# An earlier gather for the feed-forward's first group, another ring place for its first scratch, and alternating engines at each group's end

## The chip, the cores and the metric

One core of a Trainium2 chip runs the whole program in one launch. The metric is the device time of one execution in microseconds, the median of the runs shown; smaller is better. The core's engines are TensorE (PE in the profile, with PEld for its weight loads), VectorE (DVE), ScalarE (ACT), GpSimd (POOL) and the queue of SyncE (SP), which issues most of the transfers. TensorE's granted clock has two levels, 2.4 GHz (1.0 in the rows) and 1.2 GHz (0.5).

## The reference

Three stages follow each other:

```python
# 1. clustered attention: 2 batches, 8 heads, 768 positions, width 64
mask = q_assign[:, :, :, None] == k_assign[:, :, None, :]     # same nearest centroid
attn = softmax(where(mask, q @ k.T / 8, -1e9));  x = attn @ v  # -> 1536 tokens of 512
# 2. mixture of 8 experts, one per token
idx = argmax(xn @ en.T / tau);  gate = softmax(...)[idx]
out[idx == e] = gate * (relu(x[idx == e] @ w1[e]) @ w2[e])     # 512 -> 1024 -> 512
# 3. feed-forward with a rational function
h = x @ w_in;  P = a0 + a1*h + a2*h^2 + a3*h^3;  Q = 1 + |b0|*|h| + |b1|*h^2
y = (P / (Q + 1e-6)) @ w_out                                    # 512 -> 2048 -> 512
```

Tokens don't influence one another in stages 2 and 3, so their order there is free as long as each row ends at its place in the output.

## The kernel before

**Attention** fills the span up to about 300 us. It also writes every token's row and expert logits to the DRAM tensor `xd`, and `route` counts each token's rank within its expert.

**Experts.** Each expert e has 256 rows (`cap`); expert e's tokens are fetched by rank with indirect transfers (`load_x`, L842). The loop over `steps` runs eight experts in four steps (e, p) each: `expert_in` (L958), `expert_relu`, and `expert_out` of the step before (L981 to L983). After an expert's last `expert_out`, ACT scales its result into `ysb` (L987), POOL adds the token number (L71) and SP stores it to `ys_d` (L990), two stores per expert, 128 rows each. The last expert's steps are (7, 0) to (7, 3).

**Slots.** `positions` sorts the tokens by expert without gaps and computes for each of the 12 blocks of 128 sorted tokens which row of `ys_d` each token has (`slot_all`), which lanes must not be written (`never_all`), and which tokens are left over (`ovf_all`): those past rank 256 of their expert, and those among the first 512 whose expert is not covered by the first group's gather. If any is left over, a loop at the end (L1206 on) computes it again in a general way; its count is read once (`left`, L1164).

**Feed-forward.** Three groups of four blocks (512 tokens), each in 16 steps (g, f). `gather` (L996) fetches a block's rows from `ys_d` by an indirect transfer of POOL's queue; a transfer waits for the stores to the rows that its slice of `ys_d` holds. The first group's four gathers are issued after step (7, 0); `transpose_y` (L1010, copies L1012 and L1013) of its blocks stands in steps (7, 2) and (7, 3), between `expert_in` and `expert_out`. Step (0, 0) begins before the last `expert_out`. In each later step TensorE does `ff_in` (L1026, 12 matmuls) of that step and `ff_out` (L1150 to L1152, 12 matmuls) of three steps before. Between them the rational function goes around three engines: `poly_1` (ACT L1049 to L1051, DVE L1052 and L1054, POOL L1053), `poly_2` one step later (ACT L1125 and L1126, DVE L1127 to L1129), `poly_3` (ACT L1137, and L1138 on POOL in the first group, on DVE in the others). `ff_in`'s results have two PSUM places from step (0, 2) on, and L1054 is the last reader of one, so `ff_in` of step (0, f) waits for L1054 of step (0, f-2). The scratch tile `Bt` has one place: ACT's L1051 of a step waits for DVE's L1128 of the step before.

**The ring of weights.** Eight places (`ck0` to `ck7`) hold chunks of weights, split into two parts by ACT (L110) and DVE (L113). Chunk n lies in place n modulo 8. Place 4 held expert 7's first half of `w1` (chunk 28, last read in step (7, 1)) and takes the third chunk of `w_in` (chunk 36) in steps (0, 1) to (0, 3). Place 6 held expert 7's first half of `w2` (chunk 30, last read by `expert_out` of (7, 1)) and takes the fourth chunk of `w_in` (chunk 38) from step (0, 6) on. The parts of the feed-forward's chunks are made by `wide_part`, two in odd and one in even steps, after `poly_3` of the step before. Step (0, 0) runs while the experts' pools are still open, so its scratch (`spare`) is taken from the ring.

**Order.** The work is ordered by hand (`manual_schedule`); each engine runs its instructions in that order, so a waiting instruction holds all behind it on its engine.

Of the kernel before, what the change touches and what calls it, by code (L numbers as in the profile page):

```python
# [16 lines left out]
ALU = mybir.AluOpType  # L17
# [4 lines left out]
P = 128  # L22
# [6 lines left out]
def attention_moe_kernel(ctx: ExitStack, tc: tile.TileContext, kqT, vp, centroids,  # L29
                         emb, tau, w1, w2, w_in, w_out, pa, pb, out, cap=256, dbg=None):  # L30
# [7 lines left out]
    pe, act, dve, pool, sp = nc.tensor, nc.scalar, nc.vector, nc.gpsimd, nc.sync  # L38
# [4 lines left out]
    E, DM, F = w1.shape  # L43
# [10 lines left out]
    NEVER = 1 << 20  # L54
# [29 lines left out]
    oh_all = const.tile([P, NBT, E], F32, name="oh_all")  # L84
# [3 lines left out]
    slot_all = const.tile([P, NBT], I32, name="slot_all")  # L88
    never_all = const.tile([P, NBT], F32, name="never_all")
    ids = const.tile([P, E * 2], F32, name="ids")  # L90
    rank_all = stage.tile([P, NBT], F32, name="rank_all", bufs=1)
# [28 lines left out]
    def prep_f32(key, src, tag):  # L120

        raw = stage.tile([P, 4, 512], F32, name="wraw", tag="wraw")
        sp.dma_start(raw, src)
        yield
        ck = new_chunk(key, tag)
        for i in range(4):
            split_to(ck, i, raw[:, i], act, dve)
            yield
# [16 lines left out]
    RING = 8  # L145


    plan = []
# [3 lines left out]
    plan = [prep_f32(key, src, n % RING) for n, (key, src) in enumerate(plan)]  # L152
# [434 lines left out]
    n = len(units)  # L587
# [246 lines left out]
    GB = 4  # L834
# [42 lines left out]
    def positions():  # L877
        def big(name, n=E):
            return mo.tile([P, NBT, n], F32, name=name, bufs=1)

        def small(name, n=E):
            return mo.tile([P, n], F32, name=name, bufs=1)

        dve.tensor_copy(ids, row_tok)
        empty = small("pem", E * 2)
        dve.tensor_scalar(empty, ids, 0.0, float(NEVER), op0=ALU.is_equal, op1=ALU.mult)
        dve.scalar_tensor_tensor(ids, ids, -1.0, empty, op0=ALU.add, op1=ALU.add)
        pi = pX.tile([P, KC, P], F32, name="px2")[:, 0, 0:E]
        for e in range(E):
            pe.matmul(pi[:, e:E], onesb, cum[:, e:e + 1].to_broadcast([P, E - e]), start=(e == 0),  # L890
                      stop=(e == E - 1))
        inc = small("pin")
        dve.tensor_copy(inc, pi)
        yield
        more = small("pmo")
        dve.tensor_scalar(more, inc, -1.0, float(cap), op0=ALU.mult, op1=ALU.add)
        dve.tensor_tensor(more[:, 1:E], more[:, 1:E], inc[:, 0:E - 1], op=ALU.add)
        ge, gd, ex, sl = big("pge"), big("pgd"), big("pex", 1), big("psl", 1)
        dve.tensor_tensor(ge, tok.unsqueeze(2).to_broadcast([P, NBT, E]),
                          inc.unsqueeze(1).to_broadcast([P, NBT, E]), op=ALU.is_ge)  # L900
        dve.tensor_tensor(gd, ge, more.unsqueeze(1).to_broadcast([P, NBT, E]), op=ALU.mult)
        yield
        dve.tensor_reduce(ex, ge, axis=AX.X, op=ALU.add)
        dve.tensor_reduce(sl, gd, axis=AX.X, op=ALU.add)
        ex, sl = ex[:, :, 0], sl[:, :, 0]
        dve.tensor_tensor(sl, sl, tok, op=ALU.add)
        dve.tensor_scalar(slot_all[:, 0:GB], sl[:, 0:GB], float((E - 1) * cap - 1), None, op0=ALU.min)
        dve.tensor_scalar(slot_all[:, GB:], sl[:, GB:], float(ROWS - 1), None, op0=ALU.min)
        yield

        dve.scalar_tensor_tensor(sl, ex, -float(cap), sl, op0=ALU.mult, op1=ALU.add)
        dve.tensor_scalar(never_all, sl, float(cap), float(NEVER), op0=ALU.is_ge, op1=ALU.mult)
        dve.tensor_scalar(ex[:, 0:GB], ex[:, 0:GB], float(E - 1), float(NEVER), op0=ALU.is_ge, op1=ALU.mult)
        dve.tensor_tensor(never_all[:, 0:GB], never_all[:, 0:GB], ex[:, 0:GB], op=ALU.max)
        yield

        ovf_all = big("pov", 1)[:, :, 0]
        dve.tensor_scalar(ovf_all, rank_all, float(cap), None, op0=ALU.is_ge)
        dve.tensor_scalar(sl, rank_all, inc[:, E - 2:E - 1], float(GB * P), op0=ALU.add, op1=ALU.is_lt)
        dve.tensor_tensor(sl, sl, oh_all[:, :, E - 1], op=ALU.mult)  # L920
        dve.tensor_tensor(ovf_all, ovf_all, sl, op=ALU.max)
        yield
        ovb = mo.tile([P, NBT], BF16, name="povb", bufs=1)
        dve.tensor_copy(ovb, ovf_all)
        yield
        cnt = pX.tile([P, KC, P], F32, name="px2")[:, 0, 0:NBT]
        pe.matmul(cnt, onesb, ovb, start=True, stop=True)
        dve.tensor_copy(cnt_i[:, 0:NBT], cnt)
        tot = small("ptot", 1)
        dve.tensor_reduce(tot, cnt, axis=AX.X, op=ALU.add)  # L930
        dve.tensor_copy(cnt_i[:, NBT:], tot)

        dve.tensor_scalar(dst_left, ovf_all, -float(NEVER), float(NEVER), op0=ALU.mult, op1=ALU.add)
        dve.tensor_tensor(dst_left, dst_left, tok, op=ALU.add)
# [57 lines left out]
    def gather(gi, tb):  # L992
        k = gi * GB + tb
        y = rows.tile([P, W], F32, name="y", bufs=4)
        n = (E if gi else E - 1) * cap
        pool.indirect_dma_start(out=y, out_offset=None, in_=ys_d[0:n, :],  # L996
                                in_offset=bass.IndirectOffsetOnAxis(ap=slot_all[:, k:k + 1], axis=0),
                                bounds_check=n - 1, oob_is_err=False)
        x2["y", k] = y
# [31 lines left out]
    def cuts(gi, fb):  # L1031

        if (gi, fb) in ((0, 0), (NG - 1, F2B - 1)):
            return [slice(0, GT // 2), slice(GT // 2, GT)]
        return [slice(0, GT)]

    def poly_1(gi, fb):
        h = hs[gi, fb]
        if (gi, fb) == (0, 0):
            if fb == 0:  # L1040
                n = (len(plan) + 4) % RING
                hs["spare"] = pools[n].tile([P, 2, 4, 512], F32R, name="spare", tag=f"ck{n}")
            A, Bt, Ct = (hs["spare"][:, fb, k].bitcast(F32) for k in range(3))
        else:
            A = ro.tile([P, GT], F32, name="A")
            Bt = bt.tile([P, GT], F32, name="Bt", bufs=1)
            Ct = ro.tile([P, GT], F32, name="Ct", bufs=3)
        for c in cuts(gi, fb):
            act.activation(A[:, c], h[:, c], AF.Abs)  # L1049
            act.activation(Ct[:, c], h[:, c], AF.Identity, scale=ab[:, 3:4], bias=ab[:, 2:3])  # L1050
            act.activation(Bt[:, c], A[:, c], AF.Identity, scale=bb[:, 1:2], bias=bb[:, 0:1])  # L1051
            dve.tensor_tensor(Ct[:, c], Ct[:, c], h[:, c], op=ALU.mult)  # L1052
            (dve if (gi, fb) == (NG - 1, F2B - 1) else pool).tensor_tensor(Bt[:, c], Bt[:, c], A[:, c], op=ALU.mult)  # L1053
            dve.scalar_tensor_tensor(Ct[:, c], Ct[:, c], ab[:, 1:2], h[:, c], op0=ALU.add, op1=ALU.mult)  # L1054
        hs[gi, fb] = (A, Bt, Ct)

    with tc.manual_schedule():
# [6 lines left out]
        for i, (e, p) in enumerate(steps):  # L1064
# [24 lines left out]
            if e == E - 1:  # L1089
                if p == 0:  # L1090
# [4 lines left out]
                    for tb in range(GB):  # L1095
                        gather(0, tb)
        ff_in(0, 0)
        poly_1(0, 0)
        expert_out(*steps[-1])
        passed.add(("out", *steps[-1]))  # L1100
# [11 lines left out]
    gs, op = {}, {}  # L1112
# [4 lines left out]
    def scatter(y, dst, n):  # L1117
        pool.indirect_dma_start(out=outs[n][:, :], out_offset=bass.IndirectOffsetOnAxis(ap=dst, axis=0),  # L1118
                                in_=y, in_offset=None, bounds_check=NT - 1, oob_is_err=False)
# [21 lines left out]
    def ff_out(gi, fb):  # L1141
        ghi, glo = gs.pop((gi, fb))
        if fb == 0:
            op[gi] = [pR.tile([P, DM], F32, name=f"pr{tb}") for tb in range(GB)]
        w = chunks["wo", fb // 4]
        k = fb % 4
        for tb in range(GB):
            s_ = slice(tb * P, (tb + 1) * P)
            o = op[gi][tb]
            pe.matmul(o, ghi[:, s_], w[:, 0, k, :], start=(fb == 0), stop=False)  # L1150
            pe.matmul(o, ghi[:, s_], w[:, 1, k, :], start=False, stop=False)  # L1151
            pe.matmul(o, glo[:, s_], w[:, 0, k, :], start=False, stop=(fb == F2B - 1))  # L1152
            if fb == F2B - 1:
                b = gi * GB + tb
                if tb % 2 == 0:
                    op["o"] = yraw[0].tile([P, 2, DM], F32, name="yraw", bufs=3)
                y = op["o"][:, tb % 2]
                if tb >= 2:
                    dve.tensor_scalar(y, o, -1.0, None, op0=ALU.mult)
                else:  # L1160
                    act.activation(y, o, AF.Copy, scale=-1.0)
                scatter(y, dst_all[:, b:b + 1], b)
# [3 lines left out]
    with tc.manual_schedule():  # L1166
        dve.memset(qc, QC)
        steps = [(gi, fb) for gi in range(NG) for fb in range(F2B)]
        for i, (gi, fb) in enumerate(steps):
# [4 lines left out]
            if gi + 1 < NG and fb in (4, 6, 8, 10):  # L1174
                tb = (fb - 4) // 2
# [145 lines left out]
```

## Time and profile before

| | |
|---|---|
| median of 3 runs | 788.43 us (787.19 to 793.78) |
| the profiled execution | 789.97 us, span 788.2 us, mean granted clock 0.977 |
| PE busy | 740.8 us, 94% |
| PEld busy | 646.4 us, 82% |
| DVE busy | 595.9 us, 76% |
| ACT busy | 566.9 us, 72% |
| POOL busy | 351.9 us, 45% |

The shares are means over stages. The last 350 us belong to the experts' second half and the feed-forward; there PE is busy almost without a break, and what it waits for is what counts. A row of the timeline gives start, duration, engine, line, operation, output and inputs, and in brackets the engine's idle time before it and what ended that; a row with x8 is eight instructions of one kind in a stretch without others between them.

### The profile page before, as it was taken

The numbers are of one execution on the slowest core, as the hardware profiler recorded it, in microseconds if no ns is written. First come the engines' busy times: TensorE is split into PE (matmuls) and PEld (weight loads), VectorE is DVE, ScalarE is ACT, GpSimd is POOL, SyncE is SP. The second block draws the span as 40 slices with busy tenths as digits, with TensorE's granted clock in tenths as the row PEclk, the third lists the DMA queues.
The fourth block names the chain that finished last, engine by engine and source line by source line (L and its number), as shares of the span: only waits on it lengthen the run. The fifth ranks groups of instructions, "written<-read, shape, count | busy, mean of one in ns | idle before, by whom it ended". The sixth has DMA issues, their size and how long they took to land. (4 is left out here: it accounts for less than half of the span.)

```text
span 788.2 us, 12616 instructions
## 1 busy us (share of the span) xinstructions
PE 740.8 (94%) x4292; PEld 646.4 (82%) x4292; DVE 595.9 (76%) x1117; ACT 566.9 (72%) x1132; POOL 351.9 (45%) x448
## 2 busy tenths in 40 slices
PE   5999999999969976999999998989999999999995
PEld 4799999989869965889999997868888888888883
DVE  7788888889868984976765654488977878787874
ACT  3788888888868863776775554478887777777773
POOL 7497888778766522011111012156544431242211
PEclk9999999999999996999999999989999999999998
DMA  5566775877877342899655565222100200010001
GB/s 152 151 195 179 213 218 170 257 215 219 282 190 212 108 134 63 278 308 318 228 195 200 186 188 188 81 67 93 31 0 1 82 14 14 1 54 1 1 0 58
DMA packets 48313, 109.22 MB, mean 139 GB/s; under 512 B 6921, under 2 KB 10505, under 8 KB 48242
## 3 DMA queue, kind: packets, MB, share of 16 engines
q1 hardware_dynamic: 45042, 97.74, 39.8%
q0 software_dynamic: 3200, 10.60, 4.3%
q8 instruction: 36, 0.59, 0.3%
q14 instruction: 35, 0.29, 0.1%
HBM read 76.06 MB, written 18.99 MB: 121 GB/s over the span
## 5 line engine op out<-in xcount | busy, mean ns | idle before, releaser
L1053 POOL TENSOR_TENSOR Bt<-Bt,A 128x512 f32<-128x512 f32 x46 | 59.7, 1297 | 149.8 <-ACT Bt L1051 149.8
L446 DVE TENSOR_TENSOR plo<-pt,phi 128x384 fp32r<-128x384 f32 x160 | 88.0, 550 | 23.5 <-ACT phi L436 21.0
L436 ACT CAST phi<-pt 128x384 fp32r<-128x384 f32 x160 | 76.8, 483 | 35.7 <-PE pt L428 34.5
L428 PE MATMUL pt<-ident,pr 128*128 128x128 f32 x576 | 97.2, 278 | 2.6 <-DVE plo L446 2.3
L413 DVE TENSOR_REDUCE nm<-ps 128x1 f32<-128x768 f32 x96 | 91.3, 951 | 9.7 <-PE ps L411 9.2
L1026 PE MATMUL pg<-x2hi,ck 128*128 128x512 f32 x368 | 94.0, 398 | 3.2 <-DVE Ct L1054 3.2
L113 DVE TENSOR_TENSOR ck<-wraw,ck 128x512 fp32r<-128x512 f32 x128 | 82.9, 699 | 14.5 <-ACT ck L110 14.5
L419 ACT ACTIVATE pr<-ps,nm 128x768 f32<-128x768 f32 x96 | 87.5, 912 | 1.8 <-DVE nm L413 1.2
L1026 PEld LDWEIGHTS pg<-x2hi,ck 128*128 128x128 f32 x368 | 70.1, 191 | 19.3 <-DVE Ct L1054 3.6
L428 PEld LDWEIGHTS pt<-ident,pr 128*128 128x128 f32 x576 | 72.7, 142 | 14.8 <-DVE plo L446 6.7
L1150 PE MATMUL pr<-ck,ghi 128*128 128x512 f32 x192 | 76.2, 397 | 0.0
L1152 PE MATMUL pr<-ck,glo 128*128 128x512 f32 x192 | 75.4, 393 | 0.0
L110 ACT CAST ck<-wraw 128x512 fp32r<-128x512 f32 x128 | 71.2, 623 | 5.6 <-DMA wraw<-in_w_dram 5.5
L1151 PE MATMUL pr<-ck,ghi 128*128 128x512 f32 x192 | 75.1, 391 | 0.0
L410 PE MATMUL ps<-KA,QA 128*128 128x384 f32 x192 | 73.7, 384 | 1.0 <-ACT pr L419 0.6
L456 PE MATMUL po_acc<-phi,vhl 128*128 128x384 f32 x192 | 74.5, 388 | 0.0
L958 PE MATMUL ph<-xhi,ck 128*128 128x256 f32 x512 | 73.2, 286 | 0.7 <-ACT xhi L945 0.7
L958 PEld LDWEIGHTS ph<-xhi,ck 128*128 128x128 f32 x512 | 68.9, 194 | 3.7 <-ACT xhi L945 1.1
L411 PE MATMUL ps<-KB,QB 128*128 128x384 f32 x192 | 66.3, 345 | 5.0 <-DMA QB<-ot 3.4
L852 POOL TENSOR_TENSOR gss<-gss,half 128x2 f32<-128x2 f32 x8 | 5.8, 722 | 143.7 <-ACT px L851 143.7
L457 PE MATMUL po_acc<-plo,vhl 128*128 128x384 f32 x192 | 65.6, 342 | 0.0
L1127 DVE SCALAR_TENSOR_TENSOR Bt<-Bt,A 128x512 f32<-128x512 f32 (+1 forms) x48 | 32.7, 682 | 39.8 <-ACT A L1126 39.7
(252 smaller groups left out, 1848.7 us busy)
## 6 DMA issues: line engine op xcount, KB each, us to landing
wraw<-in_w_dram SPq DMA_DIRECT2D x32, 1024.0 KB, 6.2
words<-in_w_in_dram SPq DMA_DIRECT2D x16, 512.0 KB, 6.0
wf_d<-wz SPq DMA_DIRECT2D x32, 256.0 KB, 3.5
words<-in_w_out_dram SPq DMA_DIRECT2D x16, 512.0 KB, 5.0
yraw<-wf_d SPq DMA_DIRECT2D x16, 512.0 KB, 4.0
kq<-in_kqT_dram SPq DMA_DIRECT2D x16, 384.0 KB, 5.3
ys_d<-ysb SPq DMA_DIRECT2D x16, 260.0 KB, 4.7
v<-in_vp_dram SPq DMA_DIRECT2D x16, 192.0 KB, 5.3
```

The source lines that it names most:

```text
L113: el.tensor_tensor(ck[:, 1, i], src, ck[:, 0, i].bitcast(F32), op=ALU.subtract)
L413: dve.tensor_reduce(nm, ps[:, :, :HS], axis=AX.XY, op=ALU.max, negate=True)
L419: act.activation(pr.rearrange("p (a s) -> p a s", a=2), ps[:, :, :HS], AF.Exp, bias=nm[:, 0:1], accum_out=st["sum", u][:, qb:qb + 1])
L428: pe.transpose(t[:, j, :], st["P", u][j][:, kb * P:(kb + 1) * P], ident)
L436: act.copy(phi, tv)
L446: dve.tensor_tensor(plo, tv, phi.bitcast(F32), op=ALU.subtract)
L456: pe.matmul(o, w, phi, start=(kb == 1), stop=False)
L958: pe.matmul(ph[:, f2, :], w[:, wx, k, c0:c0 + P], x[:, k, :], start=(i == 0), stop=(i == len(ops) - 1))
L1026: pe.matmul(ph, w[:, wx, k, c0:c0 + P], x[:, k, :], start=(i == 0), stop=(i == len(ops) - 1))
L1150: pe.matmul(o, ghi[:, s_], w[:, 0, k, :], start=(fb == 0), stop=False)
L1151: pe.matmul(o, ghi[:, s_], w[:, 1, k, :], start=False, stop=False)
L1152: pe.matmul(o, glo[:, s_], w[:, 0, k, :], start=False, stop=(fb == F2B - 1))
```

## The change

The first group is gathered from the rows of the first six experts instead of the first seven; the clamp of its slots, its lanes that must not be written and the left-over tokens follow (a token of the first 512 whose expert is 6 or 7 is now left over; three small DVE instructions more). The scratch of step (0, 0) lies in ring place 6 instead of 4. At the end of each group the four blocks of output are negated by ACT, DVE, ACT, DVE instead of ACT, ACT, DVE, DVE.

```diff
-        dve.tensor_scalar(slot_all[:, 0:GB], sl[:, 0:GB], float((E - 1) * cap - 1), None, op0=ALU.min)
+        dve.tensor_scalar(slot_all[:, 0:GB], sl[:, 0:GB], float((E - 2) * cap - 1), None, op0=ALU.min)
...
-        dve.tensor_scalar(ex[:, 0:GB], ex[:, 0:GB], float(E - 1), float(NEVER), op0=ALU.is_ge, op1=ALU.mult)
+        dve.tensor_scalar(ex[:, 0:GB], ex[:, 0:GB], float(E - 2), float(NEVER), op0=ALU.is_ge, op1=ALU.mult)
...
-        dve.tensor_scalar(sl, rank_all, inc[:, E - 2:E - 1], float(GB * P), op0=ALU.add, op1=ALU.is_lt)
-        dve.tensor_tensor(sl, sl, oh_all[:, :, E - 1], op=ALU.mult)
-        dve.tensor_tensor(ovf_all, ovf_all, sl, op=ALU.max)
+        for e in (E - 2, E - 1):
+            dve.tensor_scalar(sl, rank_all, inc[:, e - 1:e], float(GB * P), op0=ALU.add, op1=ALU.is_lt)
+            dve.tensor_tensor(sl, sl, oh_all[:, :, e], op=ALU.mult)
+            dve.tensor_tensor(ovf_all, ovf_all, sl, op=ALU.max)
...
-        n = (E if gi else E - 1) * cap
+        n = (E if gi else E - 2) * cap
...
-                n = (len(plan) + 4) % RING
+                n = (len(plan) + 6) % RING
...
-                if tb >= 2:
+                if tb % 2:
                     dve.tensor_scalar(y, o, -1.0, None, op0=ALU.mult)
                 else:
                     act.activation(y, o, AF.Copy, scale=-1.0)
```

## Rows read from the trace of the kernel before

**Rows 1.** Waits of TensorE, 440 us to the end: us in total, times, longest.

```profile
PE pg L1026 <- DVE Ct L1054: 3.2, 1, 3.2
PE px L1010 <- DMA y<-ys_d,slot_all: 2.5, 1, 2.5
```

**Rows 2.** Timeline of TensorE, steps (7, 2) and (7, 3) of the experts.

```profile
483.38 1.10 PE L958 MATMUL ph<-xhi,ck 128*128 128x256 f32 x8
...
488.94 1.97 PE L1010 MATMUL px<-ident,y 128*128 128x128 f32 x8 [2.54 <-DMA y<-ys_d,slot_all]
...
494.24 1.10 PE L958 MATMUL ph<-xhi,ck 128*128 128x256 f32 x8
...
500.76 2.02 PE L1026 MATMUL px<-x2hi,ck 128*128 128x512 f32 x8
```

**Rows 3.** Stretches: us, busy PE, PEld, DVE, ACT, POOL, granted clock, DMA, GB/s.

```profile
489.00:492.00 3.00, 3.00 (x12) 2.71 (x13) 1.20 (x3) 1.64 (x4) 0.00 (x0) 0.50 0.44 143
...
520.00:526.00 6.00, 5.29 (x13) 4.13 (x13) 4.92 (x8) 5.15 (x9) 3.74 (x4) 0.50 0.00 0
...
349.00:356.00 7.00, 5.79 (x38) 4.98 (x38) 6.87 (x18) 5.46 (x11) 0.00 (x0) 1.00 0.68 215
```

**Rows 4.** Timeline of TensorE: `ff_in` of (0, 4), (0, 5) and (0, 10).

```profile
520.71 3.78 PE L1026 MATMUL pg<-x2hi,ck 128*128 128x512 f32 x8 [3.21 <-DVE Ct L1054]
...
529.00 2.02 PE L1026 MATMUL pg<-x2hi,ck 128*128 128x512 f32 x8
...
557.25 2.02 PE L1026 MATMUL pg<-x2hi,ck 128*128 128x512 f32 x8
```

**Rows 5.** Timeline of POOL: the first gather.

```profile
483.67 1.13 POOL L996 DMA_INDIRECT y<-ys_d,slot_all  x1 [9.03 <-DMA yraw<-wf_d]
```

**Rows 6.** Timeline of SP's queue: the stores of experts 5 and 6.

```profile
455.48 0.81 SPq L990 DMA_DIRECT2D ys_d<-ysb  x2
...
478.02 1.02 SPq L990 DMA_DIRECT2D ys_d<-ysb  x2
```

**Rows 7.** The page's DMA issues: count, KB each, median us from issue to landing.

```profile
ys_d<-ysb SPq DMA_DIRECT2D x16, 260.0 KB, 4.7
```

**Rows 8.** The gathered tile: ns min/median/max, first and last start; then us to landing.

```profile
L996 POOL DMA_INDIRECT y<-ys_d,slot_all x12: 998/1319/1348, 483.7 to 648.7; - x12
...
DMA to landing us min/median/max: 3.7/3.9/5.2
```

**Rows 9.** Timeline of DVE and of TensorE around the left-over count.

```profile
338.79 0.19 DVE L920 TENSOR_TENSOR psl<-psl,oh_all 128x12 f32<-128x12 f32 x1
...
346.84 1.89 DVE L113 TENSOR_TENSOR ck<-wraw,ck 128x512 fp32r<-128x512 f32 x3 [3.09 <-ACT ck L110]
...
351.35 0.66 PE L943 MATMUL px<-ident,xr 128*128 128x128 f32 x4 [1.22 <-DVE ptot L930]
```

**Rows 10.** Timeline of ACT: the first casts into place 4.

```profile
514.61 1.14 ACT L110 CAST ck<-yraw 128x512 fp32r<-128x512 f32 x2 [2.20 <-POOL glo L1138]
```

**Rows 11.** Timeline of POOL: `poly_3` of (0, 0).

```profile
513.15 1.43 POOL L1138 TENSOR_TENSOR glo<-spare,ghi 128x256 fp32r<-128x256 f32 x2
```

**Rows 12.** Timeline of DVE, steps (0, 1) to (0, 3), and L1054 of (0, 8).

```profile
515.26 1.29 DVE L113 TENSOR_TENSOR ck<-yraw,ck 128x512 fp32r<-128x512 f32 x2 [1.94 <-ACT ck L110]
517.07 0.69 DVE L1127 SCALAR_TENSOR_TENSOR Bt<-Bt,A 128x512 f32<-128x512 f32 x1 [0.52 <-ACT A L1126]
...
519.91 0.75 DVE L1054 SCALAR_TENSOR_TENSOR Ct<-Ct,ab,pg 128x512 f32<-128x512 f32 x1
...
525.80 2.45 DVE L113 TENSOR_TENSOR ck<-yraw,ck 128x512 fp32r<-128x512 f32 x2
...
554.84 0.75 DVE L1054 SCALAR_TENSOR_TENSOR Ct<-Ct,ab,pg 128x512 f32<-128x512 f32 x1
```

**Rows 13.** Timeline of POOL: the last group's first two output transfers.

```profile
777.36 1.01 POOL L1118 DMA_INDIRECT out_dram<-yraw,dst_all  x1 [12.09 <-ACT yraw L1161]
...
778.68 0.98 POOL L1118 DMA_INDIRECT out_dram<-yraw,dst_all  x1 [0.31 <-DVE yraw L1159]
```

## The prediction

> **What bounds the kernel now.** Read the page first: PE is busy 94% of the span, but a mean says nothing of a single stage. The forty slices show PE at eight or nine tenths in every slice from 350 us to the last but one, so there the sum of its matmuls is the time, and only what stops PE can be won. The list of TensorE's waits from 440 us to the end has two entries, one occurrence each [rows 1]: 2.5 us for the gathered rows and 3.2 us for L1054 on DVE. The change touches both.
>
> What a wait costs is more than its length, so read the timeline around each. From `expert_in` of (7, 3) at 494.24 to what follows its step at 500.76 are 6.52 us [rows 2]. The step before does the same work and starts at 483.38; undisturbed it would end at 489.90, and it ends at 494.24: **4.3 us lost**, though PE stood still for only 2.5. The rest is clock: right after the wait it is granted at 0.50, the lower level [rows 3].
>
> The second wait, 3.2 us, ends with `ff_in` of (0, 4) at 520.71; step (0, 5) starts at 529.00, 8.3 us later, and from there to (0, 10) five steps take 28.25 us, 5.65 each [rows 4]. So the wait and the clock behind it, again at 0.50 [rows 3], cost 3.2 + 2.7 = **5.9 us**.
>
> **First edit, the gather.** The stores of experts 5 and 6 are issued at 455.48 and 478.02, two each [rows 6]. POOL stands before the first gather from 474.64 to 483.67 [rows 5]. The label there names a weight transfer; but expert 6's second store, issued near 478.7, lands by the median of 4.7 us [rows 7] at 483.4, and that fits better. With six experts the last stores wanted are those of 455.48, long landed. The gathers then start near 475, take up to 1.35 us each on POOL and land within 5.2 us [rows 8]: all four by about 485.5, the first two by 482. These two are wanted when the matmuls of (7, 2) end near 486.2. POOL has nothing behind them before the scratch of (0, 0), so nothing is pushed back. PE keeps its clock and wins **4.3 us**. Bounds: 2.5, if the clock falls for another reason, to 4.3; I take 4.3, since nothing else stops PE there.
>
> What is late next: `ff_in` of (0, 0) needs the copies of the transposed rows on ACT and DVE. It ran directly behind (7, 3) before [rows 2], and that step isn't changed. No new wait.
>
> The left-over count gains three DVE instructions like L920, 0.2 us each [rows 9]. Behind them DVE stands idle 3.09 us for a cast on ACT [rows 9]; that is the cover. If it were gone, PE's wait for the count would grow from 1.22 us [rows 9] to 1.8, and with the clock lost as after the other two waits by some 1.7 more: 0 to 2.3 us. I take 0. The fallback loop stays unused as long as no token is left over: by the reference's router experts 0 to 5 have 1116 tokens, and the first 512 belong to experts 0 to 2.
>
> **Second edit, the scratch.** ACT's casts into place 4 stand idle 2.20 us [rows 10] until POOL's `glo` of (0, 0), which ends at 514.58 [rows 11], has read the scratch. Place 4's other reader is (7, 1), long past, so with the scratch in place 6 the casts can start at 512.4. Place 6 was last read on PE in (7, 2), before the scratch is written, and is wanted again from (0, 6) on: no wait appears there.
>
> How much of 2.2 us reaches PE? After the casts come ACT's two instructions of `poly_2` and DVE's chain from L1127 at 517.07 to the end of L1054 at 520.66 [rows 12], which releases PE. But DVE must first do its part of the two casts, L113. The pair takes 1.29 us alone and 2.45 us next to a `glo` on POOL (525.80) [rows 12]. Moved up it stands next to `glo` of (0, 0), from 513.15 to 514.58 [rows 11]. Held by it fully, the pair ends near 515.8, and L1127 starts 1.3 us sooner than now; not held, L1127 starts at 514.9, behind ACT, 2.2 us sooner. I take **1.4**, since the row with 2.45 is the same pair beside the same work. PE then still waits 3.2 - 1.4 = 1.8 us at (0, 4), from 517.5 to 519.3.
>
> Does the clock fall after 1.8 us? It did after 2.5 [rows 2, 3], and it did not after the 1.22 at 351 [rows 3, 9]; I take it as more likely than not, for 1.7 us. The Trainium skill ("TensorE: Matmul & The Clock Gate", section "HAM oscillation — how this bites in real kernels") warns only of idle gaps longer than either of those here. By that rule the clock would hold, and the sum below would be 0.6 us better; the row with 0.50 behind a wait of 2.5 us disagrees, and the measurement decides.
>
> From then on the chain around ACT, POOL and DVE limits. In the first group it turns about as slowly as PE: L1054 of (0, 8) ends at 555.59 [rows 12], and `ff_in` of (0, 10), which needs it, starts at 557.25 [rows 4], only 1.7 us later. If the chain moves by 1.4, this end comes at 554.2. PE, from 519.3 on, would be at (0, 10) at 519.3 + 5.6 + 28.25 = 553.2 with the clock up, and would wait 1 us there; with one fall of the clock it comes at 554.9. So (0, 10) starts 3.0 or 2.4 us sooner than now. I take **2.6**. Of the 5.9 us lost, 3.3 stay.
>
> **Third edit, the alternation.** ACT and DVE negate two blocks each as before. At the very end POOL issues the output transfers 1.3 us apart, beginning with the first block's [rows 13], and that block stays with ACT; DVE has until 778.7 for the second. In the inner groups the same instructions run beside `ff_in` of the next group. **0**; if ACT had to stand before the third block for the three matmuls of 0.23 us that finish it, 0.7 us at each of three ends, hidden there by POOL's spacing and, in the later groups, by PE's lead.
>
> **Sum.** 4.3 + 2.6 = 6.9 us. The profiled execution took 789.97 us (span 788.2), so 783.1; it lies 1.5 above the median of 788.43. Against the median: **781.5 us**, 0.9% less.
>
> **Rivals.**
> *The second wait hardly shrinks.* DVE's L113 and POOL's `glo` hold each other up until nearly all is eaten, and the clock falls for as long as now. For it: 2.45 against 1.29. Against: ACT's 2.20 idle are really gone. 4.3 + 0.3 to 1 gives 783.5.
> *The second loss goes wholly.* If L113 isn't held, PE waits 1.0 us and keeps its clock. With the 1.7 us of lead at (0, 10) the chain allows 1.7 + 2.2 = 3.9, so 780.2; if the chain itself closes up, 5.9, so 778.2. Against: the row of 2.45.
> *The gather isn't freed.* Its memory or another transfer of the label holds it until about 483. Against: it started just when expert 6's store must have landed. Only 2.6 remain: 785.8.
> *Slower.* The four early gathers, 0.27 MB each, now run while loads of feed-forward weights are fetched. ACT's casts of such loads stand ahead of `expert_relu` of (7, 2) and of the copies of the transposed rows. If loads slipped by about 6 us, those copies would come later than `ff_in` of (0, 0) wants them, and every further microsecond stops PE; the whole gain is eaten at a slip of some 13, and at 15 the time is 790. Against: at 143 GB/s the engines were busy 0.44 of the time [rows 3], so they can move some 325, and the gathers' 1.1 MB take 3.3 us.
>
> **Numbers.** The forecast's mechanism, with gains of 5.8 to 8.2, has 0.65; the second wait hardly shrinking 0.16; the second loss wholly gone 0.10; the gather not freed 0.05; slower 0.04. A measurement here tells about 1% (7.9 us) from no change. With the spread of the median's runs a third of the forecast's case lies beyond that: 0.23 + 0.10 makes 0.33 for faster, 0.63 for the same, 0.04 for slower. The range reaches from the loss wholly gone to the wait that hardly shrinks, with 1.5 us for the spread of a median at that end: 778.5 to 785.
>
> **What would show it.** In the new profile PE has no wait for gathered rows, (7, 2) and (7, 3) take 6.5 us each with the clock at 1.0, and the first gather starts about 1 us behind POOL's `ysb` copies. ACT's casts into place 4 follow `ghi` with no wait for POOL, and L113 beside `glo` takes over 2 us for the pair. PE's wait before (0, 4) is near 1.8 us, and one near 1 us may stand before (0, 10). From (0, 11) to the end all is as before, 6.9 us sooner. The forecast is wrong if a wait of PE appears at (0, 0), if the chain between (0, 4) and (0, 10) changes its pace, or if the instructions of ACT around (0, 0) come in another order.

## The result and the profile after

| | before | after |
|---|---|---|
| median | 791.49 us (20 runs, 787.05 to 799.37) | 782.95 us (20 runs, 780.82 to 793.6) |
| ratio | | 0.990, 95% interval 0.988 to 0.9919 |
| span of the profiled execution | 788.2 us | 781.3 us |
| mean granted clock | 0.977 | 0.982 |

The change saves 1.0%, where the forecast was 0.9% (781.5 against 788.43 us); the median lies in the range of 778.5 to 785. The ratio counts fast runs alone, and the run of 793.6 us after is a slow one. Behind the three added instructions the line numbers after L920 are one higher than before.

The waits of TensorE from 440 us to the end, after (us in total, times, longest), which answer to [rows 1]. The wait for gathered rows is gone, and the other is down from 3.2 us to two short ones:

```profile
PE pg L1027 <- DVE Ct L1055: 2.4, 2, 1.6
```

The timeline of TensorE in steps (7, 2) and (7, 3), after, beside [rows 2]. From 484.23 to 490.76 are 6.53 us, as long as (7, 3) itself, and the transposes (L1011) start with no idle time in brackets:

```profile
484.23 1.10 PE L959 MATMUL ph<-xhi,ck 128*128 128x256 f32 x8
...
487.09 1.04 PE L1011 MATMUL px<-ident,y 128*128 128x128 f32 x8
...
490.76 1.11 PE L959 MATMUL ph<-xhi,ck 128*128 128x256 f32 x8
...
497.30 2.02 PE L1027 MATMUL px<-x2hi,ck 128*128 128x512 f32 x8
```

The timeline of TensorE, `ff_in` of (0, 4) and of (0, 10), after, beside [rows 4]. Waits of 1.63 and 0.81 us are left:

```profile
515.67 2.13 PE L1027 MATMUL pg<-x2hi,ck 128*128 128x512 f32 x8 [1.63 <-DVE Ct L1055]
...
550.59 2.12 PE L1027 MATMUL pg<-x2hi,ck 128*128 128x512 f32 x8 [0.81 <-DVE Ct L1055]
```

Stretches of the kernel after around these places: us, busy PE, PEld, DVE, ACT, POOL, granted clock, DMA, GB/s. The clock is 1.00 in all three, where [rows 3] had 0.50 behind both waits:

```profile
485.00:492.00 7.00, 7.00 (x50) 6.45 (x50) 3.83 (x9) 4.20 (x11) 0.00 (x0) 1.00 0.46 183
513.00:520.00 7.00, 5.37 (x24) 4.04 (x23) 5.87 (x9) 5.59 (x9) 3.29 (x3) 1.00 0.22 75
549.00:556.00 7.00, 6.19 (x29) 4.76 (x28) 6.86 (x11) 5.92 (x10) 3.92 (x4) 1.00 0.00 0
```

The timeline of POOL, after: the first gather follows the copies into `ysb` (L71) at once, where it stood 9.03 us in [rows 5]; `glo` of (0, 0) takes 1.89 us, not the 1.43 of [rows 11]:

```profile
475.14 0.34 POOL L71 TENSOR_SCALAR ysb<-ids 128x8 f32<-128x8 f32 x2
475.65 1.13 POOL L997 DMA_INDIRECT y<-ys_d,slot_all  x1 [0.17 <-issue]
...
509.69 1.89 POOL L1139 TENSOR_TENSOR glo<-spare,ghi 128x256 fp32r<-128x256 f32 x2
```

ACT's cast that waits for the load of a feed-forward weight around (7, 2): the timeline of ACT in the kernel before, then in the kernel after. The cast starts 1.29 us behind the start of (7, 2) in the first and 2.92 us behind it in the second (up to 4.33 in other executions with the earlier gathers), since the load lands later:

```profile
484.67 0.62 ACT L110 CAST ck<-yraw 128x512 fp32r<-128x512 f32 x1 [2.26 <-DMA yraw<-wf_d]
...
487.15 0.62 ACT L110 CAST ck<-yraw 128x512 fp32r<-128x512 f32 x1 [3.90 <-DMA yraw<-wf_d]
```

The timeline of ACT, after, beside [rows 10]: the casts into the third chunk follow `ghi` with no wait:

```profile
508.24 0.71 ACT L1138 CAST ghi<-spare 128x256 fp32r<-128x256 f32 x2
508.84 1.15 ACT L110 CAST ck<-yraw 128x512 fp32r<-128x512 f32 x2
```

The timeline of DVE, after, beside [rows 12]: the pair of L113 takes 2.35 us instead of 1.29, L1128 follows at once, and L1055 of (0, 2) releases TensorE:

```profile
509.77 2.35 DVE L113 TENSOR_TENSOR ck<-yraw,ck 128x512 fp32r<-128x512 f32 x2
512.04 0.68 DVE L1128 SCALAR_TENSOR_TENSOR Bt<-Bt,A 128x512 f32<-128x512 f32 x1
...
514.87 0.75 DVE L1055 SCALAR_TENSOR_TENSOR Ct<-Ct,ab,pg 128x512 f32<-128x512 f32 x1
```

To put a number on each part, the starts of the same matmuls were read from every trace: from `expert_in` of (7, 2) to that of (7, 3); from `ff_in` of (0, 0) to that of (0, 13); and from there to the last matmul. These differences don't carry what runs differ by before 310 us, where the first expert's matmuls started anywhere between 300.6 and 306.6 us after the first matmul, whatever the kernel, nor the scatter of 1.6 us between there and (7, 1).

| kernel | (7, 2) | (0, 0) to (0, 13) | to the last |
|---|---|---|---|
| before | 10.85 | 74.04 | 203.35 |
| the change | 6.53 | 70.92 | 203.32 |
| the change, second and third profile | 6.53, 6.53 | 70.89, 70.90 | 203.35, 203.34 |
| gather alone | 6.53 | 74.18 | 203.34 |
| scratch alone | 11.58 | 70.94 | 203.30 |
| alternation alone | 10.68 | 72.98 | 203.31 |
| before, with useless matmuls | 10.00 | 72.82 | 203.34 |
| no casts at (0, 1) | 6.53 | 70.41 | 203.33 |
| single casts | 6.53 | 74.00 | 203.32 |
| `glo` on DVE | 6.53 | 70.54 | 203.35 |
| third chunk early | 6.53 | 69.68 | 203.30 |
| and the product on DVE | 6.53 | 69.08 | 203.32 |
| and the last part in (7, 3) | 6.53 | 68.36 | 203.35 |

So the change saves 4.32 us in the first stretch, 3.12 in the second, nothing in the third: 7.4 us. The first number depends on the execution that it is compared with: of the three profiles that gather as before and add no work, (7, 2) takes from 10.68 to 11.58 us, as the gathered rows come sooner or later, so the same edit gives 4.2 to 5.1 us.

### The profile page after: what moved, and what is told of

Same layout as the page of the kernel before. It is cut to its first block, busy times and chain, and to the rows that moved or that the text cites. A ratio compares the mean times of both kernels' runs of the same rounds, so it can differ in the third digit from the quotient of the medians.

```text
span 781.3 us, 12623 instructions
## 1 busy us (share of the span) xinstructions
PE 736.7 (94%) x4292; PEld 643.2 (82%) x4292; DVE 597.3 (76%) x1120; ACT 566.2 (72%) x1132; POOL 352.2 (45%) x448
## 5 line engine op out<-in xcount | busy, mean ns | idle before, releaser
L1054 POOL TENSOR_TENSOR Bt<-Bt,A 128x512 f32<-128x512 f32 x46 | 59.6, 1296 | 146.5 <-ACT Bt L1052 146.5
L113 DVE TENSOR_TENSOR ck<-wraw,ck 128x512 fp32r<-128x512 f32 x128 | 82.3, 694 | 14.4 <-ACT ck L110 14.4
L1128 DVE SCALAR_TENSOR_TENSOR Bt<-Bt,A 128x512 f32<-128x512 f32 (+1 forms) x48 | 32.7, 682 | 37.3 <-ACT A L1127 37.0
```

What stands on the lines that cost most here:

```text
L113: el.tensor_tensor(ck[:, 1, i], src, ck[:, 0, i].bitcast(F32), op=ALU.subtract)
```

## The experiments

### One edit at a time

**Gather alone**: the changed kernel with the other two edits undone.

```diff
-                n = (len(plan) + 6) % RING
+                n = (len(plan) + 4) % RING
...
-                if tb % 2:
+                if tb >= 2:
```

> The first edit alone. My theory: TensorE no longer waits for gathered rows, (7, 2) takes 6.5 us as (7, 3) does, and 4.3 us are won, a ratio of 0.9945 to the kernel before. The wait of 3.2 us before (0, 4) stays as it was, with the clock at 0.50 behind it, and there is no wait before (0, 10). Rival, that something else than expert 6's stores held the gather: the wait for gathered rows stays, ratio 1.000. Rival, that the two waits share one cause and the second shrinks once the first is gone: wait before (0, 4) under 2.5 us and ratio below 0.992.

Measured: 785.24 us, ratio 0.9915 (0.9889 to 0.9942). The wait for gathered rows is gone, and the other stands as before, with the clock's loss behind it. Waits of TensorE from 440 us on, and the stretch behind the second, in this kernel:

```profile
PE pg L1027 <- DVE Ct L1055: 3.2, 1, 3.2
```

```profile
521.00:524.00 3.00, 3.00 (x8) 2.32 (x8) 2.95 (x5) 2.93 (x5) 2.04 (x2) 0.50 0.00 0
```

The gather is worth 4.32 us. That would be a ratio of 0.9945, just outside the interval; the table shows no other stretch that got shorter, so the rest is put down to nothing in particular. The ratio alone would fit the second rival (below 0.992), but the wait before (0, 4) is still 3.2 us, where that rival wanted it under 2.5.

**Scratch alone**: the kernel before with this one line.

```diff
-                n = (len(plan) + 4) % RING
+                n = (len(plan) + 6) % RING
```

> The second edit alone. My theory: ACT's first casts into place 4 follow ghi with no wait for POOL, DVE's pair L113 takes over 2 us beside glo, the wait before (0, 4) falls from 3.2 to about 1.6 us with the clock at 1.0 behind it, and a wait under 1 us appears before (0, 10): 3.0 us won, ratio 0.996. The wait for gathered rows of 2.5 us stays, with the clock at 0.50 behind it. Rival, that the chain gives the gain back later or needs the earlier gather: under 1 us won, ratio 0.999 or more. Rival, that the whole second loss goes: 5.9 us, ratio 0.9925.

Measured: 791.82 us, ratio 0.9988 (0.9955 to 1.0021), no difference that the timing can tell; 3.1 us are 0.9961, inside the interval, and so is the 0.999 of the first rival. The stretch decides: 70.94 us, as in the whole change. Waits of TensorE from 440 us on in this kernel, and the clock behind the wait of 3.5 us (ended at 495.33) and around the one of 1.63:

```profile
PE px L1010 <- DMA y<-ys_d,slot_all: 3.5, 1, 3.5
PE pg L1026 <- DVE Ct L1054: 2.4, 2, 1.6
```

```profile
496.00:498.00 2.00, 2.00 (x10) 1.81 (x9) 0.80 (x3) 1.25 (x3) 0.00 (x0) 0.50 0.11 44
520.00:526.00 6.00, 4.37 (x19) 3.24 (x19) 5.80 (x8) 4.51 (x8) 3.13 (x4) 1.00 0.27 87
```

**Alternation alone**: the kernel before with this one line.

```diff
-                if tb >= 2:
+                if tb % 2:
```

> The third edit alone. My theory: nothing, ratio 1.000 within 0.001; both waits of TensorE as before, the last output transfer issued at the same distance from the last matmul. Rival, that ACT's place in the third block helps at the ends: up to 0.7 us at each of three ends, ratio 0.997. Rival, that ACT stands before the third block: ratio 1.002.

Measured: 793.25 us, ratio 1.0007 (0.9974 to 1.0041). The stretch to the last matmul, which holds the ends of the first two groups, is the same to 0.05 us. The third group's end lies behind it, and there the expectation was missed by a little: POOL issues the last output transfer 3.24 us behind the start of the last matmul (779.41), where it was 3.43 before (778.15). POOL's timeline in the kernel before, then in this one:

```profile
781.58 0.97 POOL L1118 DMA_INDIRECT out_dram<-yraw,dst_all  x1 [0.64 <-issue]
...
782.65 0.97 POOL L1118 DMA_INDIRECT out_dram<-yraw,dst_all  x1 [0.43 <-issue]
```

It is 3.21 to 3.25 us in the ten profiles with the alternation and 3.42 to 3.44 in the four without, so 0.2 us sooner, for a reason that the profile doesn't name; from the last matmul to the end of the span profiles differ by more than that (9.4 to 10.4 us). The second stretch is 1.1 us shorter than before's with the same wait of 3.2 us, for a reason that is not the edit: the clock behind it fell for less time. From 524 to 527 (one microsecond behind the wait's end at 523.08) it shows

```profile
524.00:527.00 3.00, 3.00 (x9) 2.32 (x9) 2.29 (x4) 2.52 (x5) 0.80 (x1) 0.60 0.00 0
527.00:530.00 3.00, 3.00 (x14) 2.44 (x13) 2.96 (x4) 2.97 (x6) 2.94 (x2) 1.00 0.03 5
```

In (7, 2) this execution waited for gathered rows twice, 1.57 and 0.60 us, with four transposes between. The clock fell behind the two, and the step took 10.68 us, 4.15 more than undisturbed for 2.2 us of waiting. TensorE's timeline and the stretch behind:

```profile
490.49 0.66 PE L1010 MATMUL px<-ident,y 128*128 128x128 f32 x4 [1.57 <-DMA y<-ys_d,slot_all]
491.74 0.66 PE L1010 MATMUL px<-ident,y 128*128 128x128 f32 x4 [0.60 <-DMA y<-ys_d,slot_all]
```

```profile
493.00:495.00 2.00, 2.00 (x6) 1.56 (x5) 1.94 (x5) 1.58 (x4) 0.00 (x0) 0.50 0.13 52
```

**The whole change again**, twice, beside the kernels above and below.

> The changed kernel itself on this chip. If the edits' gains are independent, the ratio is the sum of the three others: 4.3 + 3.0 + 0 = 7.3 us, 0.991. If the second needs the first (or the other way), it is more than 0.5 us below the sum.

> The changed kernel beside the two before it, for a comparison on one chip: ratio 0.990 to 0.993, waits of 1.6 and 0.8 us.

Measured: 785.62 us, ratio 0.9928 (0.9898 to 0.9958), and 783.49 us, ratio 0.9905 (0.9873 to 0.9938), with the same waits (1.63 and 0.8) and stretches within 0.03 us of the first profile's. The two ratios are 0.0023 apart, 1.8 us, for the same code: what an edit of that size is worth, the stretches tell and the ratios can't. By the stretches the gains add up: 4.32 of the gather and 3.10 of the scratch alone, 7.44 together.

### What a wait costs beyond its length

**Useless matmuls in the wait**: the kernel before, with eleven matmuls on weights already there ahead of the transposes in (7, 2). Nothing reads their result.

```diff
+                if p == 2:
+                    idle = pX.tile([P, KC, P], F32, name="px2").rearrange("p k t -> p (k t)")
+                    wd = chunks["wi", 0]
+                    for m in range(11):
+                        pe.matmul(idle, wd[:, 0, m % 4, 0:P], wd[:, 0, m % 4, :], start=(m == 0), stop=(m == 10))
                 if p > 1:
```

> The kernel before with eleven matmuls of 128x512 added on TensorE in (7, 2) right before the transpositions, into a PSUM tile that nobody reads: useless work of 2.6 us in place of idling. My theory, that 1.7 of the 4.3 us at the first wait are the lower clock behind it: the clock stays at 1.0 in (7, 2) and (7, 3), the wait for gathered rows falls under 1 us, and from the start of (7, 2) to the start of (7, 3) it takes 9.2 to 9.5 us with no slow matmuls behind, against 10.9 before, though more is done. Rival, that the slow matmuls belong to the gathered rows' arrival and not to the idling before: they are slow here too.

Measured: 788.75 us in one run, beside 789.92 for the kernel before. The timeline of TensorE in (7, 2):

```profile
486.76 2.68 PE L1078 MATMUL px<-ck 128*128 128x512 f32 x11
489.88 1.38 PE L1010 MATMUL px<-ident,y 128*128 128x128 f32 x8 [0.45 <-DMA y<-ys_d,slot_all]
491.02 0.48 PE L981 MATMUL py<-ck,hhi 128*128 128x512 f32 x1
...
493.90 1.12 PE L958 MATMUL ph<-xhi,ck 128*128 128x256 f32 x8
```

From 486.76 to 489.88 TensorE did nothing useful, 3.12 us, longer than the 2.54 it waited before. Yet the step takes 10.00 us instead of 10.85: without that time 6.88, against 8.31 (10.85 - 2.54) before and 6.53 undisturbed. It is more than the 9.2 to 9.5 expected. The rows came 6.0 us behind the step's start in this execution and 5.6 before, and the 0.35 us over 6.53 sit in the transposes, which take 1.14 us to the matmul behind (489.88 to 491.02) and 0.79 in the kernel after. Behind them the matmuls run at full pace, 2.88 us to the next step as in the kernel after, and the clock stood at 1.00, against the rival:

```profile
490.00:494.00 4.00, 3.90 (x21) 3.16 (x22) 2.80 (x7) 2.73 (x5) 0.00 (x0) 1.00 0.37 112
```

So of the 4.3 us about 1.8 (8.31 - 6.53) belonged to the clock behind the idling, and not to the gathered rows' arrival.

### Where the rest of the second loss sits

**No casts at (0, 1)**: the two parts of the third chunk that the step makes are made later instead.

```diff
-                wide_part(2 if i % 2 else 1)
+                wide_part(0 if i == 1 else 2 if i % 2 else 1)
```

> The changed kernel with the two parts of weights that are cast and split at step (0, 1) made later (none at (0, 1), the rest in the old rhythm). My theory: of the wait of 1.6 us left before (0, 4), the part that DVE's pair L113 adds beside POOL's glo goes: L1128 of (0, 1) follows ACT's Exp, some 0.8 us sooner, and the wait falls to about 0.8 us; the wait before (0, 10) stays near 0.8 us, since the chain and TensorE move together. Rival, that the rest of the wait is the ring of ACT, POOL and DVE alone: it stays at 1.6 us.

Measured: 782.39 us in one run. The wait before (0, 4) falls from 1.63 to 0.86, that before (0, 10) grows from 0.81 to 1.16, more than was expected. DVE's L1128 now waits for ACT; with no L113 beside it `glo` takes 1.44 us:

```profile
511.15 0.69 DVE L1128 SCALAR_TENSOR_TENSOR Bt<-Bt,A 128x512 f32<-128x512 f32 x1 [1.40 <-ACT A L1127]
```

```profile
509.58 1.44 POOL L1139 TENSOR_TENSOR glo<-spare,ghi 128x256 fp32r<-128x256 f32 x2
```

The casts' place in (0, 1) holds 0.77 us of the wait; the 0.86 left belong to something else, which the section "A version without waits" takes apart. In the stretch only 0.5 us are won, since the wait before (0, 10) takes a part back.

**`glo` of (0, 0) on DVE**, so that no POOL instruction stands beside L113.

```diff
-            (pool if gi == 0 else dve).tensor_tensor(glo[:, c]
+            (pool if gi == 0 and fb else dve).tensor_tensor(glo[:, c]
```

> The changed kernel with glo of step (0, 0) on DVE instead of POOL, the casts where they are. My theory: DVE's pair L113 falls from 2.35 to about 1.3 us because POOL reads nothing beside it, but DVE's two more instructions of 0.5 us take that up: the wait before (0, 4) stays within 0.3 us of 1.6. Rival, that the pair takes over 2 us because of ACT's casts or its place: it stays over 2 us, and the wait grows by about 1 us, to 2.6.

Measured: 783.15 us in one run; the waits are 1.23 and 0.87. DVE's timeline:

```profile
510.56 0.76 DVE L1139 TENSOR_TENSOR glo<-spare,ghi 128x256 fp32r<-128x256 f32 x2
511.23 1.29 DVE L113 TENSOR_TENSOR ck<-yraw,ck 128x512 fp32r<-128x512 f32 x2
512.43 0.68 DVE L1128 SCALAR_TENSOR_TENSOR Bt<-Bt,A 128x512 f32<-128x512 f32 x1
```

The pair is back at 1.29 us: POOL's `glo` was what stretched it. Of the 1.06 us that this gives (2.35 - 1.29), 0.67 go to `glo` itself on DVE (510.56 to 511.23), and 0.40 reach the wait, so it ends just below the 1.3 to 1.9 us expected.

**Single casts**: one part instead of two in most odd steps as well.

```diff
-                wide_part(2 if i % 2 else 1)
+                wide_part(0 if i == 1 else 2 if i in (3, 5, 11) else 1)
```

> As the one before, and one part instead of two in the steps (0, 7), (0, 9), (0, 13) and (0, 15), so that no pair of L113 lies ahead of (0, 8) and (0, 10). My theory: before (0, 4) 0.8 us are left, and the wait before (0, 10) goes, since L1055 of (0, 8) ends over 1 us sooner against the steps before. Rival, that the wait before (0, 10) comes from the copies of transposed rows in the chain: it stays near 0.8 us.

Measured: 791.32 us in one run, nothing won. The waits before (0, 4) and (0, 10) fall to 0.86 and 0.54, but in (0, 12) a new one stands, since the fourth chunk's parts came too late for it. That is the spacing of this experiment, and speaks for neither theory. TensorE's timeline and the clock behind:

```profile
569.06 2.19 PE L1027 MATMUL pg<-x2hi,ck 128*128 128x512 f32 x5 [2.36 <-ACT ck L110]
```

```profile
570.00:572.00 2.00, 2.00 (x6) 1.54 (x6) 2.00 (x2) 0.78 (x2) 0.95 (x1) 0.50 0.04 8
```

(0, 12) takes 10.17 us instead of 6.01: 4.2 lost to a wait of 2.36, nearly the price of the gathered rows'.

### A version without waits

**Third chunk early**: on top of the change the experts' last steps make the third chunk too, and the feed-forward begins its parts later.

```diff
-                wide_part(3, 4)
+                wide_part(3, 5)
...
-        wide_part(2, 4)
+        wide_part(2, 5)
...
-                wide_part(2 if i % 2 else 1)
+                wide_part(i > 1)
```

> The changed kernel, and the third chunk of w_in split before the feed-forward's steps begin (three parts in (7, 3), one behind ff_in of (0, 0)), which place 4 allows now that the scratch doesn't lie there; the twelve parts left are made one a step from (0, 2) on, never in pairs. My theory: before (0, 4) 0.86 us are left, as with no casts at (0, 1); the wait before (0, 10) goes, and no wait for a chunk appears: 1.6 us sooner than the changed kernel from (7, 2) to (0, 10), 8.9 sooner than before, ratio 0.989. Rival, that the early casts stand for their loads and hold up ACT before poly_1 of (0, 0): ACT's first instruction of (0, 0) comes later than 3.0 us behind ff_in's start, and the wait before (0, 4) is over 1.6 us.

Measured: 782.47 us, ratio 0.9881 (0.9838 to 0.9923). The wait before (0, 10) is gone, no chunk is waited for, but 1.50 us stay before (0, 4), more than was expected. The likely reason is on ACT, and the last run below tests it: the chunk's last part is cast ahead of Exp (L1127), which starts the chain:

```profile
504.92 1.26 ACT L988 ACTIVATE ysb<-py,gate 128x512 f32<-128x512 f32 x2
506.06 0.63 ACT L110 CAST ck<-yraw 128x512 fp32r<-128x512 f32 x1
506.57 0.43 ACT L1127 ACTIVATE spare<-spare 128x256 f32<-128x256 f32 x1
```

**And the product on DVE**: as well, the product of step (0, 1) that POOL makes moves ahead of DVE's own.

```diff
+            if (gi, fb) == (0, 1):
+                dve.tensor_tensor(Bt[:, c], Bt[:, c], A[:, c], op=ALU.mult)
             dve.tensor_tensor(Ct[:, c], Ct[:, c], h[:, c], op=ALU.mult)
-            (dve if (gi, fb) == (NG - 1, F2B - 1) else pool).tensor_tensor(Bt[:, c], Bt[:, c], A[:, c], op=ALU.mult)
+            if (gi, fb) != (0, 1):
+                (dve if (gi, fb) == (NG - 1, F2B - 1) else pool).tensor_tensor(Bt[:, c], Bt[:, c], A[:, c], op=ALU.mult)
```

> As the one before, and the product Bt*A of step (0, 1) on DVE ahead of DVE's own L1053, instead of on POOL. My theory: what is left before (0, 4) is the ring of Bt through ACT, POOL and DVE; the product is done some 0.6 us sooner, and so is the chain behind it: 0.2 to 0.3 us left before (0, 4), ratio 0.988. Rival, that another link limits (ACT's Ln behind ghi, or Exp): the wait stays at 0.86 us.

Measured: 780.62 us, ratio 0.9882 (0.9829 to 0.9935); one wait, 0.86 us before (0, 4), where less was expected. The product gave 0.64 us, about the 0.6 forecast, but from the 1.50 of the kernel before it and not from 0.86; that the rival named 0.86 as well is chance. The cast ahead of Exp was still there.

**And the last part in (7, 3)**:

```diff
-                wide_part(3, 5)
+                wide_part(3 + (e == E - 1 and p == 3), 5)
```

> This is the kernel of the run with the third chunk early and the product on DVE, with the chunk's last part made in step (7, 3) and no longer behind the last scaling, where its cast (0.63 us, 0.51 of ACT's time) and its L113 (0.69 us) stood ahead of poly_2 of step (0, 0). Theory (the chain from ACT's Exp of (0, 0) through DVE's unbroken run of instructions to L1058 of (0, 2) sets the wait before (0, 4)): Exp starts 0.5 us sooner, so the wait falls from 0.86 to 0.35 us, the clock stays up, and the stretch from (0, 0) to past (0, 10) gets 0.5 us shorter (53.1 instead of 53.6 us). Rival (the wait is set by something else, such as POOL or the load of the raw part, which now stands before the store of the last rows on SP's queue): the wait stays at 0.8 to 0.9, or a new wait appears in (7, 3). Time against the kernel before: ratio 0.987 to 0.988; half a microsecond against the kernel without this edit can't be told from the ratio, only from the stretch.

Measured: 781.17 us, ratio 0.9861 (0.9831 to 0.9890). TensorE has no wait left in the list from 440 us to the end, and the stretch is 68.36 us, 0.72 below the one above, a little more than was expected, as DVE's L113 no longer stands ahead of the chain either. The whole stretch from `ff_in` of (0, 0) on:

```profile
499.00:565.00 66.00, 65.86 (x289) 53.27 (x288) 52.74 (x83) 54.35 (x92) 35.97 (x29) 1.00 0.22 69
```

This version beats the change by 2.56 us in the stretch (70.92 - 68.36). Between their ratios, 0.9861 and 0.9900, the intervals overlap.

## Why the prediction was right, and where it was not

**The time, 781.5 us: partly luck.** Against the 791.49 us of 20 runs the base of three runs, 788.43, was 3.1 us too low, and the gain between the medians, 8.5 us, is 1.6 over the 6.9 forecast; the two errors partly cancel in 782.95. The stretches show 7.4 us and the ratio 7.9; the rest is scatter of the runs.

**The gather, 4.3 us: shown.** Undoing the rest leaves 4.32 in (7, 2); the step takes 6.53 us in all ten profiles with this edit. Both halves hold: the gathers start behind `ysb`'s copies, and the clock stays up; the useless matmuls show that 1.8 of it was the clock's. `ff_in` of (0, 0) follows (7, 3) at once, with no new wait. A margin had been judged too wide: the four gathers landed 6.8 us after issue (up to 8.2 in another execution), not within the 5.2 of [rows 8] (the row below, of the gathered tile in the kernel after, 470 to 492 us); the third and fourth are wanted only in (7, 3), and the second, issued at 477.09, landed 3 us before 487.09.

```profile
DMA to landing us min/median/max: 6.8/6.8/6.8
```

**The three instructions of the count, 0.** The idle time on DVE that covers them is 2.48 us after, against 3.09 in [rows 9]. TensorE's wait for the count was 0.4 to 1.2 us in four profiles without them (mean 0.9) and 0.3 to 1.7 in the ten with them (mean 1.3); the stretch from the first expert's matmuls to (7, 1) is on average 0.5 us longer with them, with a scatter of 1.6, and the ranges overlap. A cost of up to half a microsecond is neither shown nor excluded.

**The scratch, 2.6 taken, 3.1 found.** The chain was sized well. TensorE's release at (0, 4) came 1.58 us sooner (18.32 us from `ff_in` of (0, 0) to the end of L1055, against 19.90), where 1.4 was taken; the wait left is 1.63, not 1.8; that before (0, 10) is 0.81, where about 1 was foreseen; and the pair of L113 took 2.35 us, where the row with 2.45 had been taken. From the end of L1055 of (0, 2) to that of (0, 8) are 34.9 us before and after, so the chain kept its pace, as the working had it. The step that failed is **"Does the clock fall after 1.8 us? ... more likely than not"**: after 1.63 it did not fall, in three profiles of the change and one of the scratch alone. The working's other branch, 3.0, was the right one, 0.4 us above the 2.6 taken (the prediction says 0.6, which is the distance to 2.4). The price of the second loss comes out at 5.7 us (74.04 less the 68.36 of the version without waits), where 5.9 was worked out. The Trainium skill ("TensorE: Matmul & The Clock Gate", section "HAM oscillation — how this bites in real kernels") warns only of idle gaps longer than any of these four waits: 1.63, 2.36, 2.5 and 3.2 us. By that rule the clock would hold after each of them; after 1.63 it did, and after the other three it fell to 0.50, so the rule doesn't order these rows, and the measurement decides.

What the scratch is worth also depends on the execution that it is compared with. The wait of 3.2 us cost the stretch 74.04 and 74.18 us in two profiles and 72.98 and 72.82 in two others, as the clock stayed down longer or shorter. So it gives 3.1 or 2.0 us.

**The alternation, 0: shown** to 0.05 us up to the last matmul. Behind it the last output transfer is issued 0.2 us sooner, which the prediction had put at nothing.

**The rivals.** L113 and `glo` did hold each other up (2.35 and 1.89 us), but not until nearly all was eaten. The second loss didn't go wholly: that took three edits more (2.56 us). The gather was freed. A load did slip, as the slower rival said: ACT's cast that waits for it starts 2.9 to 4.3 us behind the start of (7, 2) in the ten profiles with the earlier gathers and 0.6 to 1.3 in the four without, and `expert_relu` of that step comes 0.9 to 2.3 us later. That is a slip of at most 3.8 us, short of the about 6 that the rival needed, and TensorE shows nothing of it. The sum, 7.4 us, is 0.5 over the 6.9, nearly all of it the clock step's.

**The chances.** The larger chance, 0.63 for a gain too small to tell (under 1%), rested on a forecast of 0.9%; the measured 1.0% lies on the bound itself, with an interval on both sides of it, so the result speaks neither for it nor for the 0.33 on faster.

## What to carry to other kernels

Price a wait of the bounding engine by the distance between the same instructions before and behind it, not by its length: here 2.4 to 2.5 us of waiting in one piece cost 4.2 to 4.3, waits of 1.57 and 0.60 close together 4.15, and one of 1.63 no more than itself. So shortening a wait can win more than the time waited, and where it stops doing so has to be read from the traces. When single edits are worth less than the runs scatter, compare such distances in the traces: they agreed within 0.03 us where whole ratios differed by 0.2%. Work that nothing waits for soon, like the making of a later weight chunk, should not stand ahead of the instruction that starts the chain the engine waits for.

## What the runs showed of the hardware

From 440 us on the clock was granted at 0.50 after idle times of 2.36, 2.5, 3.2 and 3.5 us of an otherwise busy TensorE, and after 1.57 and 0.60 with four matmuls between; it stayed at 1.00 after single ones of 1.50 and 1.63. The loss behind a fall was 1.6 to 2.0 us in three profiles of (7, 2), and 2.5 or 1.3 behind the same wait of 3.2 us (74.04 or 72.82 less the 3.2 and the undisturbed 68.36). What decides between these the runs don't show.

Two instructions of DVE and two of POOL that each read two tiles met in (0, 1) and held each other up: alone 1.29 and 1.43 us, 2.72 in sum, together 2.43 (509.69 to 512.12). The Trainium skill ("SBUF — State Buffer", section "Who interferes with whom") says that a DVE instruction with two inputs in SBUF contends with a GpSimd instruction that reads SBUF, and that the lock is exclusive. By that the two pairs would take 2.72 us or more; the rows come near it but show 0.3 less, so they bear out that the two contend, and not that one waits for the whole of the other.
